# Joining the key tiles of the attention denominators on VectorE, and a later place for one denominator product

## The chip, the cores and the metric

The kernel runs on one NeuronCore of one Trainium2 chip. The metric is device time in microseconds (us): the median of several runs of the whole kernel, inputs and outputs in the chip's main memory. Smaller is better.

## The reference, cut to what matters

A forgetting attention (causal, with a decay made from the forget gates `f`) is followed by a two-layer MLP with a tanh GELU.

```
B, H, S, D = 8, 8, 576, 64;  scale = 1 / sqrt(64)
scores = scale * q @ k.T                        # per batch and head, 576 x 576
cum    = cumsum(log(clip(f, 1e-4, 1)))          # along the sequence
scores = where(causal, -1e9, scores + cum[query] - cum[key])
attn   = softmax(scores);  y = attn @ v         # y: (8, 8, 576, 64)
x      = y.transpose(0, 2, 1, 3).reshape(4608, 512)
out    = gelu_tanh(x @ w_in) @ w_out            # 512 -> 2048 -> 512, float32 out
```

In a row of the softmax the factor `exp(cum[query])` cancels. What is left is a weight per key, `w[key] = exp(-cum[key] - 64)`, on the exponential of the plain score: the output is `sum_k w[k] P[k,q] v[k] / sum_k w[k] P[k,q]` with `P = exp(scale * k.q)`, zero above the diagonal.

## The kernel before, in words

**Tiles.** The 64 pairs of batch and head are handled as 16 *quads* of 4 heads; quads 2b and 2b+1 belong to batch b. Keys lie on the 128 partitions, queries on the free axis, so `P` is stored transposed in `pt` (two buffers, quad i uses `pt[i % 2]`), 1536 columns a head: key tile 0 (keys 0-127) for queries 64-575, tile 1 for queries from 128 (448 columns), tile 2 from 256 (320 columns), tile 3 from 384 (192 columns), and one block of 64 columns that holds two halves, "low" (the first 64 keys for the first 64 queries) and "high" (the last 64 keys for the last 64 queries).

**One quad.** `scores` (L202-228) runs in three rounds of 512 columns; each fills two PSUM tiles of the pool `psS` (2 buffers) with matmuls of 32 rows, four heads side by side, and ScalarE writes the exponentials into `pt`, two heads at a time (L228). `mask` (L230-247) zeroes above the diagonals with `affine_select` on GpSimd (POOL). `make_vw` (L174-180) multiplies the values by `w`, also on POOL, behind the mask of round 1; `copy_low` (L182) copies a part of it on VectorE. `denominators(i)` (L297-313) multiplies `pt` by the weights `w_bf`: the function `product` (L266-293) issues 6 pieces x 4 heads = 24 matmuls, with four heads side by side on the columns of the array, and `den`, `rec`, `rb` on VectorE (transpose, reciprocal, transpose) turn the sums into factors. The columns streamed are 512 + 64 + 448 + 320 + 192 + 64 = 1600 a head. `attn_out(i, x)` (L315-319), twice a quad, is the same product with the 32 even or odd columns of the weighted values, and VectorE multiplies it by `rb` into `xT`. All these products use one PSUM buffer, `psO` (1 buffer), so each has to wait until VectorE has read the one before.

**The MLP.** It works on 9 chunks of 512 rows of `x`. `mlp_in` (L322-337) does 8 x 8 matmuls of 512 columns and a GELU on ScalarE; `mlp_out` (L357-376) is a generator that yields after each of 4 x 16 *parts* (a part is one 128-row step of a 128 x 512 output, here as four 32-column matmuls side by side). After every 16 parts VectorE copies the output tile to `o_st` (L373) and SyncE's queue stores it; `psM` has 2 buffers.

**The order** is written by hand; nothing plans it. Each engine takes its own instructions in program order. `setup` and the table `FRONT` handle quads 0-6; then the loop (L551-565) does, for chunk c from 2 to 6, first what is left of the output of chunk c-1, then the 8 groups of `mlp_in(c)` with `prepare` (transposes of q and k on VectorE and their next loads on POOL's queue) behind the second group, then 6 parts of output and `pair(i, j, c)` with i = 2c+3 and j = 2c+2. In `pair` (L524-536), which interleaves attention with parts of the output of chunk c, the order on TensorE is as follows (S = a score round, D = denominators, V = an output product, a number = parts of `mlp_out`, k = i+1):

```
S.i.0 D.j 12  S.i.1 V.j.0 10  S.i.2 V.j.1 9
S.k.0 D.i 10  S.k.1 V.i.0 5 V.i.1 4  S.k.2          (8 parts are left for the next chunk)
```

In the last pair (i = 15) there is no k: `S.i.0 D.j 12 S.i.1 V.j.0 10 S.i.2 V.j.1 9 D.i 10 V.i.0 V.i.1 10`.

Of the kernel before, what the change touches and what calls it, by code (L numbers as in the profile page):

```python
# [8 lines left out]
FP32 = mybir.dt.float32  # L9
BF16 = mybir.dt.bfloat16  # L10
AF = mybir.ActivationFunctionType
ALU = mybir.AluOpType
# [4 lines left out]
def kernel(  # L17
# [10 lines left out]
    nc = tc.nc  # L28

    B, H, S, D = q.shape  # L30
    BH = B * H
    NT = (S + 127) // 128
    LAST = S - 128 * (NT - 1)
# [7 lines left out]
    NQ = BH // 4  # L41
# [4 lines left out]
    CH = 512  # L46
    NCH = B * S // CH
    ZW = 64

    rounds = [(0, 512), (512, 512), (1024, 512)]  # L50
    pieces = [
# [28 lines left out]
        S.4.1 m.3.1 LQ.6 F.0.6 TQ.5 H.4.2.1 D.3 H.4.0.1 LQ.7 VW.4 H.4.0.0 V.3.1 v.3.0 f.0.3 H.4.2.0 CL.4 I.1.0 m.4.1 LV.2.1@LQ.5 I.1.5  # L80
        TQ.6 m.4.2.3 I.1.1 I.1.7 LV.3.0@LQ.7 m.4.2.2 TK.6 M.4.0 I.1.3 I.1.2 I.1.4 I.1.6 X F.1.8 S.5.0 F.1.2 F.1.14 S.5.1 D.4 M.5.0 f.1.9
        S.5.2 V.4.0 m.5.2.3 f.1.6 VW.5 V.4.1 CL.5 m.5.2.2 LQ.8 S.6.0 f.1.6 M.5.1 D.5 f.1.4 S.6.1 V.5.1 f.1.7 V.5.0 vw.6 S.6.2
        m.6.1 M.6.2.2 m.6.0 m.6.2.3 LK.7 LK.8 CL.6 LX.3.1@LK.6
    """

    singles = ctx.enter_context(tc.tile_pool(name="singles", bufs=1))
    ostage_pool = ctx.enter_context(tc.tile_pool(name="ostage", bufs=3))
# [5 lines left out]
    def many(n, shape, dtype, name):  # L93
        return [singles.tile(shape, dtype, name=f"{name}{i}") for i in range(n)]
# [19 lines left out]
    before = singles.tile([128, (NT - 1) * BH], FP32, name="before")  # L114
    wT = singles.tile([128, NQ, NT, 4], FP32, name="wT")
    w_bf = singles.tile([128, NQ, NT + 1, 4], BF16, name="w_bf")
    shift = singles.tile([128, 1], FP32, name="shift")
    idle = singles.tile([128, 512], BF16, name="idle")
    spare = singles.tile([1, 1], FP32, name="spare")
# [82 lines left out]
    def scores(i, r, groups=((0, 1, 2, 3),)):  # L202

        qq, p = qT[i % 2], pt[i % 2]
        if i < 2:
            off, n = split_rounds[r]
            todo = [(key, col - off, q0, nq) for (key, col, q0, nq) in split_pieces[r]]
        else:
            off, n = rounds[r]
            todo = []  # L210
            for (key, col, q0, nq) in pieces:
                a, z = max(col, off), min(col + nq, off + n)
                if a < z:
                    todo.append((key, a - off, q0 + a - col, z - a))
        for heads in groups:
            tiles = {g: psS.tile([128, 2, 512], FP32, name="ps_s", tag="s") for g in sorted({h // 2 for h in heads})}
            for c in range(2):
                for j, (key, c0, q0, nq) in enumerate(todo):
                    for h in heads:
                        nc.tensor.matmul(  # L220
                            tiles[h // 2][:, h % 2, c0:c0 + nq],
                            key_columns(i, key, h, c),
                            qq[32 * h:32 * h + 32, q0:q0 + nq, c],
                            start=(c == 0 and j == 0), stop=(c == 1),
                            skip_group_check=True,
                        )
            for g, t in tiles.items():
                nc.scalar.activation(p[:, 2 * g:2 * g + 2, off:off + n], t[:, :, 0:n], AF.Exp, scale=scale)  # L228
# [37 lines left out]
    def product(i, groups, spare, part=None):  # L266
        p = pt[i % 2]
        if part is not None:
            s0, s1 = parts[part]
            po = psM.tile([128, 512], FP32, name="po_m", tag="m")  # L270
            for (key, col, q0, nq) in sorted(sum(split_pieces[1:] if part else split_pieces[:1], []), key=lambda x: HIGH if x[0] == "high" else x[0]):
                for (r0, lhsT, h) in groups:
                    w = lhsT(HIGH if key == "high" else key)
                    nc.tensor.matmul(  # L274
                        po[r0:r0 + w.shape[-1], q0 - s0:q0 - s0 + nq], w, p[:, h, col:col + nq],
                        start=(key == 0), stop=(key == (HIGH if part else 1)),
                        skip_group_check=True,
                    )
            return po[:, 0:s1 - s0]
        if spare:  # L280
            po = psS.tile([128, 2, 512], FP32, name="ps_o", tag="s").rearrange("p a n -> p (a n)")
        else:
            po = psO.tile([128, 1024], FP32, name="po", tag="po")
        for (key, col, q0, nq) in sorted(pieces, key=lambda x: {0: 0, "low": 1}.get(x[0], 2)):
            t = {"low": LOW, "high": HIGH}.get(key, key)
            for (r0, lhsT, h) in groups:
                w = lhsT(t)
                nc.tensor.matmul(  # L288
                    po[r0:r0 + w.shape[-1], 448 + q0:448 + q0 + nq], w, p[:, h, col:col + nq],
                    start=(key in (0, "low")), stop=(key in ("low", "high")),  # L290
                    skip_group_check=True,
                )
        return po[:, 448:448 + S]

    rbs = {}

    def denominators(i, part=None):  # L297

        def column(h):

            return lambda t: (w_bf[:, i, t, h:h + 1] if t not in (0, LOW) else
                              w_bf[:, i, t, h:h + 1].to_broadcast([128, 32]))

        po = product(i, [(32 * h, column(h), h) for h in range(4)], False, part)
        n = S if part is None else parts[part][1] - parts[part][0]
        den = den_pool.tile([128, S], FP32, name="den", tag="den")
        nc.vector.transpose(out=den[:, 0:n], in_=po)  # L307
        rec = den_pool.tile([128, S // 32], FP32, name="rec", tag="rec")
        nc.vector.reciprocal(rec[:, 0:n // 32], den[:, 0:n:32])
        rb = den_pool.tile([128, S], FP32, name="rb", tag="rb")  # L310
        nc.vector.transpose(out=rb[:, 0:n].rearrange("p (c j) -> p c j", j=32),  # L311
                            in_=rec[:, 0:n // 32].unsqueeze(2).to_broadcast([128, n // 32, 32]))
        rbs[i, part] = rb[:, 0:n]

    def attn_out(i, x, spare=False, part=None):  # L315
        b, u = i // QPB, i % QPB
        po = product(i, [(32 * h, lambda t, h=h: vw[i % 2][:, t, h, x:D:2], h) for h in range(4)], spare, part)
        s0, s1 = (0, S) if part is None else parts[part]
        nc.vector.tensor_mul(xT[:, 2 * u + x, S * b + s0:S * b + s1], po, rbs[i, part])  # L319
# [106 lines left out]
    def make_w():  # L426
# [3 lines left out]
        for (rows, t0, t1) in ((128, 0, HIGH), (64, HIGH, NT)):  # L430
# [2 lines left out]
                cum_ps[:rows, t0 * BH:t1 * BH].rearrange("p (t i h) -> p t i h", i=NQ, h=4),  # L433
                AF.Exp, scale=-1.0, bias=shift[:rows, :])

    by_columns = []

    def pull(it, n):
# [7 lines left out]
    def out_part(c, n, tiled=0):  # L446
        by_columns[:] = [True] * tiled
        pull(fills.setdefault(c, mlp_out(c)), n)
# [5 lines left out]
    def load_values(b, half):  # L454
# [33 lines left out]
        "F": out_part,  # L488
        "f": lambda c, n: out_part(c, n, 1),
        "B": keep_busy,  # L490
        "X": load_exp,
    }

# [11 lines left out]
    def beside(i, r, c, todo):  # L505

        if i is not None:
            scores(i, r)
        for n, x in enumerate(todo):
            if isinstance(x, int):  # L510
                out_part(c, x, 1)
            else:
                x()
            if n == 0 and i is not None:
                after_scores(i, r)

    def after_scores(i, r):
        mask(i, r)
        if r == 1:
            make_vw(i, nc.gpsimd)  # L520
        if r == 2:
            copy_low(i)

    def pair(i, j, c):  # L524

        D, V = (lambda q: lambda: denominators(q)), (lambda q, x, spare=False: lambda: attn_out(q, x, spare))
        beside(i, 0, c, [D(j), 12])
        beside(i, 1, c, [V(j, 0), 10])
        beside(i, 2, c, [V(j, 1), 9])
        if i + 1 < NQ:  # L530
            beside(i + 1, 0, c, [D(i), 10])
            beside(i + 1, 1, c, [V(i, 0), 5, V(i, 1), 4])
            scores(i + 1, 2)
            after_scores(i + 1, 2)
        else:
            beside(None, 0, c, [D(i), 10, V(i, 0), V(i, 1, True), 10])

    def prepare(*quads):

        for i in quads:  # L540
            if i < NQ:
                transpose_k(i)
                transpose_q(i)
                if i + 2 < NQ:
                    load_one(k, k_c, i + 2)
                    load_one(q, q_c, i + 2)

    with tc.manual_schedule():
        setup()
        run(FRONT)  # L550
        for c in range(2, NCH):  # L551
            out_part(c - 1, CH)
            for pr in range(2):
                mlp_in(c, (pr,))
            if c + 1 < B:
                prepare(2 * c + 3, 2 * c + 4)
            if c + 2 < B:
                load_v(c + 2)
            for pr in range(2, NP):
                mlp_in(c, (pr,))  # L560
            if c + 1 < B:
                load_exp()
                out_part(c, 6)
                pair(2 * c + 3, 2 * c + 2, c)
        out_part(NCH - 1, CH)
# [30 lines left out]
```

## Time and profile before

| what | value |
|---|---|
| median of 3 runs | 341.61 us (341.45 to 345.22) |
| span of the profiled execution | 339.9 us, first to last instruction |
| around the span (median less span) | 1.7 us |
| TensorE (PE) busy | 329.8 us, 97% |
| VectorE (DVE) busy | 132.3 us, 39% |
| ScalarE (ACT) busy | 191.8 us, 56% |
| GpSimd (POOL) busy | 110.1 us, 32% |
| granted TensorE clock | 1.000 |

The page of the profile has, besides the busy time of each engine, the span cut into 40 slices with the busy tenths of each engine, the chain of work that ended last, and the costliest groups of instructions. The timeline of one engine gives start, duration, line, operation and `out<-in` of its instructions, neighbours of one kind merged (x3 stands for three instructions), and in brackets how long the engine sat idle before them and for whom. Durations of one instruction overlap with the next one's by the time an engine takes to drain, so the distance from start to start is shorter than the duration. The page gives the span of the profiled execution and no separate total for it; sums are made against the span of 339.9 us, and the 1.7 us around it are taken as they are.

### The profile page before, as it was taken

Reading aid. Unit: us, or ns where it says so; the run is one execution under the profiler, and the core shown is the slowest. Engines: PE = TensorE matmul, PEld = TensorE weight load, DVE = VectorE, ACT = ScalarE, POOL = GpSimd, SP = SyncE. Lnnn points to the kernel's source line nnn. Section 1 sums busy time; section 2 is a strip of 40 time slices with the busy share of each in tenths; the row PEclk is TensorE's granted clock in tenths of the full one; section 3 lists DMA queues with packets and bytes.
Section 4 is the critical chain, followed back from the end, with each engine's and each line's share of the span. In section 5 each row is a group of like instructions: output and inputs, shape, how many; then the busy total and the mean of one; then the engine's idle time right before and its main releaser. Section 6 shows DMA issues by size and latency. Waiting matters only on the chain.

```text
span 339.9 us, 9423 instructions
## 1 busy us (share of the span) xinstructions
PE 329.8 (97%) x4241; PEld 162.0 (48%) x4241; DVE 132.3 (39%) x206; ACT 191.8 (56%) x201; POOL 110.1 (32%) x155
## 2 busy tenths in 40 slices
PE   3999999999999999999999999999999999999996
PEld 1458844544454445444444444444544454444443
DVE  4686059830465435703462244413430450021011
ACT  4784686677547665667566665674576624502510
POOL 8987551600506233601551145106410410000000
PEclk9999999999999999999999999999999999999999
DMA  7999999570316970591129210910100010011012
GB/s 127 207 216 214 196 230 194 102 172 2 95 36 101 227 156 33 131 205 39 35 77 207 59 67 35 212 30 35 63 31 2 33 63 34 2 62 62 0 40 85
DMA packets 40201, 33.26 MB, mean 98 GB/s; under 512 B 27473, under 2 KB 29777, under 8 KB 40161
## 3 DMA queue, kind: packets, MB, share of 16 engines
q0 software_dynamic: 8848, 16.58, 27.4%
q1 hardware_dynamic: 31168, 16.01, 17.0%
q8 instruction: 33, 0.54, 0.7%
q10 hardware_dynamic: 144, 0.07, 0.1%
q14 instruction: 8, 0.06, 0.0%
HBM read 36.85 MB, written 9.44 MB: 136 GB/s over the span
## 4 chain that ended last, share of the span: by engine, by line
PE 90%; DMA 2%; POOL 2%; ACT 2%; DVE 1%; issue 1%; POOLq 0%; DVEq 0%; ACTq 0%
PE pso L368 36%; PE ps_h L330 33%; PE po L288 8%; PE ps_s L220 8%; PE ps_h L347 4%; DMA v_nat<-in_v_dram 2%; ACT pt L228 2%; PE po_m L274 1%; POOL vw L178 1%; POOL v_nat L132 0%; PE ps_o L288 0%; DVE pt L263 0%; DVE vw L178 0%; POOL pt L234 0%; POOL q_c L155 0%
## 5 line engine op out<-in xcount | busy, mean ns | idle before, releaser
L368 PE MATMUL pso<-w_out_sb,gT 128*32 128x512 bf16 (+3 forms) x1492 | 134.5, 377 | 0.0
L228 ACT ACTIVATE pt<-ps_s 128x1024 bf16<-128x1024 f32 (+2 forms) x100 | 93.7, 988 | 53.6 <-PE ps_s L220 46.0
L330 PE MATMUL ps_h<-xT,w_in_sb 128*128 128x512 bf16 x512 | 111.9, 379 | 0.0
L337 ACT ACTIVATE gT<-ps_h 128x1024 bf16<-128x1024 f32 x64 | 65.5, 1024 | 64.1 <-PE ps_h L330 64.1
L234 POOL TENSOR_SCALAR_AFFINE_SELECT pt<-pt 128x512 bf16<-128x512 bf16 (+3 forms) x65 | 38.2, 597 | 140.6 <-ACT pt L228 139.7
L368 PEld LDWEIGHTS <-gT 128*32 128x32 bf16 (+1 forms) x1492 | 56.3, 97 | 56.8 <-issue 3.5
L330 PEld LDWEIGHTS <-w_in_sb 128*128 128x128 bf16 x512 | 50.0, 98 | 60.4 <-issue 0.4
L373 DVE COPY o_st<-pso 128x512 f32<-128x512 f32 (+2 forms) x37 | 24.9, 673 | 71.8 <-PE pso L368 71.5
L307 DVE STREAM_TRANSPOSE den<-po 128x576 f32<-128x576 f32 x14 | 11.0, 784 | 65.7 <-PE po L288 65.7
L220 PE MATMUL ps_s<-qT,kT 32*128 32x64 bf16 (+5 forms) x896 | 36.2, 264 | 0.2 <-ACT pt L228 0.2
L319 DVE TENSOR_TENSOR xT<-po,rb 128x576 bf16<-128x576 f32 x26 | 19.7, 757 | 31.6 <-PE po L288 31.5
L178 POOL TENSOR_TENSOR vw<-v_nat,wT 128x1280 bf16<-128x1280 f32 (+1 forms) x13 | 30.0, 2308 | 0.1
L220 PEld LDWEIGHTS <-kT 32*128 32x128 bf16 x896 | 16.4, 93 | 23.7 <-issue 18.8
L161 DVE STREAM_TRANSPOSE kT<-k_c 128x576 f32<-128x576 f32 x16 | 20.0, 1248 | 16.9 <-DMA k_c<-in_k_dram 16.8
L288 PE MATMUL po<-pt,vw 128*32 128x64 bf16 (+4 forms) x624 | 22.4, 278 | 0.0
L161 DVE STREAM_TRANSPOSE qT<-q_c 128x576 f32<-128x576 f32 x16 | 19.9, 1244 | 1.2 <-PE ps_s L220 0.7
L288 PEld LDWEIGHTS <-vw 128*32 128x32 bf16 x672 | 14.2, 97 | 11.8 <-issue 3.7
L132 POOL DMA_DIRECT2D v_nat<-in_v_dram x20 | 15.3, 776 | 3.4 <-DMA w_out_sb<-in_moe_w_out_dram 3.4
L347 PE MATMUL ps_h<-xT,w_in_sb 128*128 128x256 bf16 x128 | 14.5, 273 | 0.0
L347 PEld LDWEIGHTS <-w_in_sb 128*128 128x128 bf16 x128 | 12.3, 98 | 1.7
L311 DVE STREAM_TRANSPOSE rb<-rec 128x576 f32<-128x576 f32 (+2 forms) x18 | 12.8, 711 | 0.6
L155 POOL DMA_DIRECT2D k_c<-in_k_dram x16 | 9.1, 568 | 11.3 <-DVE kT L161 5.7
(61 smaller groups left out, 124.9 us busy)
## 6 DMA issues: line engine op xcount, KB each, us to landing
out_dram<-o_st SPq DMA_DIRECT2D x35, 256.0 KB, 2.1
k_c<-in_k_dram POOLq DMA_DIRECT2D x16, 288.0 KB, 6.8
q_c<-in_q_dram POOLq DMA_DIRECT2D x16, 288.0 KB, 7.4
v_nat<-in_v_dram SPq DMA_DIRECT2D x16, 256.0 KB, 8.3
w_in_sb<-in_moe_w_in_dram POOLq DMA_DIRECT2D x4, 512.0 KB, 9.5
w_out_sb<-in_moe_w_out_dram POOLq DMA_DIRECT2D x4, 512.0 KB, 7.2
v_nat<-in_v_dram SPq DMA_DIRECT2D x16, 128.0 KB, 3.3
v_nat<-in_v_dram POOLq DMA_DIRECT2D x13, 128.0 KB, 7.9
```

Source lines behind the costliest of these rows:

```text
L161: nc.vector.transpose(out=dst.rearrange("p s c -> p (s c)").bitcast(FP32) .rearrange("p (t a) -> p a t", a=S // 32), in_=src.rearrange("p ...
L178: eng.tensor_mul(vw[i % 2][:, t0:t1], vb[:, t0:t1, h0:h0 + 4, :], wT[:, i, t0:t1, :].unsqueeze(3).to_broadcast([128, t1 - t0, 4, D]))
L220: nc.tensor.matmul(tiles[h // 2][:, h % 2, c0:c0 + nq], key_columns(i, key, h, c), qq[32 * h:32 * h + 32, q0:q0 + nq, c], start=(c == 0 an ...
L228: nc.scalar.activation(p[:, 2 * g:2 * g + 2, off:off + n], t[:, :, 0:n], AF.Exp, scale=scale)
L234: nc.gpsimd.affine_select(out=x, in_=x, compare_op=ALU.is_ge, fill=0.0, base=0, pattern=pattern, channel_multiplier=-1)
L288: nc.tensor.matmul(po[r0:r0 + w.shape[-1], 448 + q0:448 + q0 + nq], w, p[:, h, col:col + nq], start=(key in (0, "low")), stop=(key in ("lo ...
L319: nc.vector.tensor_mul(xT[:, 2 * u + x, S * b + s0:S * b + s1], po, rbs[i, part])
L330: nc.tensor.matmul(ph[:, j, :], w_in_sb[:, dt, 128 * ft:128 * ft + 128], xT[:, dt, CH * c:CH * (c + 1)], start=(dt == 0), stop=(dt == N_DT ...
L337: nc.scalar.activation(gT[c % 2][:, 2 * pr:2 * pr + 2, :], ph, AF.Gelu_apprx_tanh)
L347: nc.tensor.matmul(ph[:, j // 2, QA * (j % 2):QA * (j % 2) + QA], w_in_sb[:, dt, 128 * ft:128 * ft + 128], xT[:, dt, n0:n0 + QA], start=(d ...
L368: nc.tensor.matmul(pso[c0:c0 + cols, m0:m1], gT[c % 2][:, ft, 128 * n + c0:128 * n + c0 + cols], w_out_sb[:, ft, m0:m1], start=(ft == 0), ...
L373: nc.vector.tensor_copy(st[:, m0:m1], pso[:, m0:m1])
```

## The change

From quad 6 on, VectorE forms sums over key tiles before TensorE sees them. With `ratio[t] = w[tile t] / w[tile t+1]` per partition, `fold = P0 * ratio[0] + P1` is a tile for which the weight of tile 1 alone is enough; the same is done with tile 2 and tile 3 in place. `folded_sums` then multiplies each query range once, by the last tile that it has: 64 + 64 + 128 + 128 + 192 + 64 = 640 columns a head where there were 1600. Each fold of a quad is 4 instructions (one a head) of 448, 320 and 192 columns in turn. The even quads fold in the next chunk, ahead of `prepare`; the odd quad i of a pair folds inside the pair, and in the last pair only tile 0 is joined with tile 1 (1152 columns). All weights are now spread to 32 columns. `D.i` moves from behind S.k.0 to behind S.k.1, the parts are dealt out anew (none is left for the next chunk), and `V.i.1` moves behind S.k.2. In the new order below, E is a fold (E.i.0.0.1: quad i, tile 0 into 1, heads 0 and 1), and A is what follows a score round (mask, `make_vw`, `copy_low`).

```diff
+    PAIR = """
+        S.i.0 D.j A.i.0 12 S.i.1 V.j.0 A.i.1 E.i.0.0.1 10 S.i.2 V.j.1 A.i.2 E.i.0.2.3 9
+        S.k.0 E.i.1 E.i.2 A.k.0 12 S.k.1 D.i 6 V.i.0 A.k.1 6 S.k.2 V.i.1 A.k.2 4
+"""
+    LAST = """
+        S.i.0 D.j A.i.0 12 S.i.1 V.j.0 A.i.1 E.i.0.0.1 10 S.i.2 V.j.1 A.i.2 E.i.0.2.3 9
+        D.i 10 V.i.0 v.i.1 10
+"""
...
+    def fold_keys(i, t, heads=range(4)):
+        p, a = pt[i % 2], fold[i % 2]
+        q0, col = 128 * (t + 1), {0: 576, 1: 1024, 2: 1344}[t]
+        n = S - q0
+        for h in heads:
+            nc.vector.scalar_tensor_tensor(
+                a[:, h, q0 - 128:], p[:, h, 128:128 + n] if t == 0 else a[:, h, q0 - 128:],
+                ratio[:, i, t, h:h + 1], p[:, h, col:col + n], op0=ALU.mult, op1=ALU.add)
+        folded[i] = t + 1
+
+    def folded_sums(i, column, levels):
+        p, a = pt[i % 2], fold[i % 2]
+        po = psO.tile([128, 1024], FP32, name="po", tag="po")
+        todo = [(LOW, p[:, :, 0:64], 0), (0, p[:, :, 64:128], 64)]
+        for (t, q0, col, n) in ((1, 128, 576, 448), (2, 256, 1024, 320), (3, 384, 1344, 192)):
+            if t > levels:
+                todo.append((t, p[:, :, col:col + n], q0))
+            else:
+                z = S if t == levels else q0 + 128
+                todo.append((t, a[:, :, q0 - 128:z - 128], q0))
+        todo.append((HIGH, p[:, :, 0:64], 512))
...
     def denominators(i, part=None):
+        wide = range(NT + 1) if i in folded else (0, LOW)
...
-        po = product(i, [(32 * h, column(h), h) for h in range(4)], False, part)
+        if i in folded:
+            po = folded_sums(i, column, folded[i])
+        else:
+            po = product(i, [(32 * h, column(h), h) for h in range(4)], False, part)
...
+    def make_ratio():                 # once, at the end of FRONT
+        r = ratio[:, FOLD:]           # FOLD = 6
+        nc.vector.reciprocal(r, wT[:, FOLD:, 1:NT - 1, :])
+        nc.vector.tensor_mul(r, r, wT[:, FOLD:, 0:NT - 2, :])
...
             if c + 1 < B:
+                for t in range(3):
+                    fold_keys(2 * c + 2, t)
                 prepare(2 * c + 3, 2 * c + 4)
```

More of the change, by code (lines that the diff above doesn't have):

```diff
@@ L48 @@
     ZW = 64
+    FOLD = 6
     rounds = [(0, 512), (512, 512), (1024, 512)]
@@ L82 @@
         S.5.2 V.4.0 m.5.2.3 f.1.6 VW.5 V.4.1 CL.5 m.5.2.2 LQ.8 S.6.0 f.1.6 M.5.1 D.5 f.1.4 S.6.1 V.5.1 f.1.7 V.5.0 vw.6 S.6.2
-        m.6.1 M.6.2.2 m.6.0 m.6.2.3 LK.7 LK.8 CL.6 LX.3.1@LK.6
+        m.6.1 M.6.2.2 m.6.0 m.6.2.3 LK.7 LK.8 CL.6 LX.3.1@LK.6 RA
     """
+    PAIR = """
[6 more added lines that the diff above has]
+"""
     singles = ctx.enter_context(tc.tile_pool(name="singles", bufs=1))
@@ L116 @@
     w_bf = singles.tile([128, NQ, NT + 1, 4], BF16, name="w_bf")
+    ratio = singles.tile([128, NQ, NT - 2, 4], FP32, name="ratio")
+    fold = many(2, [128, 4, S - 128], BF16, "fold")
     shift = singles.tile([128, 1], FP32, name="shift")
@@ L295 @@
     rbs = {}
+    folded = {}
+    def fold_keys(i, t, heads=range(4)):
[18 more added lines that the diff above has]
+        todo.append((HIGH, p[:, :, 0:64], 512))
+        for j, (t, x, q0) in enumerate(todo):
+            for h in range(4):
+                w = column(h)(t)
+                nc.tensor.matmul(
+                    po[32 * h:32 * h + w.shape[-1], 448 + q0:448 + q0 + x.shape[-1]], w, x[:, h, :],
+                    start=(j < 2), stop=(j in (0, len(todo) - 1)), skip_group_check=True)
+        return po[:, 448:448 + S]
     def denominators(i, part=None):
+        wide = range(NT + 1) if i in folded else (0, LOW)
         def column(h):
-            return lambda t: (w_bf[:, i, t, h:h + 1] if t not in (0, LOW) else
+            return lambda t: (w_bf[:, i, t, h:h + 1] if t not in wide else
                               w_bf[:, i, t, h:h + 1].to_broadcast([128, 32]))
-        po = product(i, [(32 * h, column(h), h) for h in range(4)], False, part)
+        if i in folded:
+            po = folded_sums(i, column, folded[i])
+        else:
+            po = product(i, [(32 * h, column(h), h) for h in range(4)], False, part)
         n = S if part is None else parts[part][1] - parts[part][0]
@@ L490 @@
         "B": keep_busy,
+        "RA": make_ratio,
         "X": load_exp,
@@ L524, in pair @@
     def pair(i, j, c):
[L526 to L536, printed above, removed]
+        last = i + 1 == NQ
+        for word in (LAST if last else PAIR).split():
+            name, *args = word.split(".")
+            if name.isdigit():
+                out_part(c, int(name), 1)
+                continue
+            q, *args = args
+            q = {"i": i, "j": j, "k": i + 1}[q]
+            args = list(map(int, args))
+            if name == "A":
+                after_scores(q, *args)
+            elif name == "E":
+                fold_keys(q, args[0], args[1:] or range(4))
+            else:
+                ops[name](q, *args)
     def prepare(*quads):
```

## The prediction

> **What bounds the kernel now.** First the page: busy time, then the chain that ended last.
>
> ```profile
> span 339.9 us, 9423 instructions
> PE 329.8 (97%) x4241; PEld 162.0 (48%) x4241; DVE 132.3 (39%) x206; ACT 191.8 (56%) x201; POOL 110.1 (32%) x155
> ...
> PE 90%; DMA 2%; POOL 2%; ACT 2%; DVE 1%; issue 1%; POOLq 0%; DVEq 0%; ACTq 0%
> ```
>
> TensorE is the bound, without gaps from pair to pair, so a column taken from it is a gain, and any wait put before it is a loss at full price. VectorE's 39% hides nothing by itself: what matters is where in a pair its work stands. So I read one pair, (i, j) = (11, 10), in the chain (start, duration, what):
>
> ```profile
> 190.37 0.62 PE ps_s L220 x20
> 190.99 0.80 PE po L288 x24
> 191.79 2.59 PE pso L368 x48
> ...
> 201.20 0.63 PE ps_s L220 x21
> 201.83 0.80 PE po L288 x24
> 202.63 2.16 PE pso L368 x40
> 204.78 0.57 PE ps_s L220 x16
> ```
>
> A product (`po`, 24 matmuls) costs 0.80 behind a score round, 12 parts 2.59 (0.216 a part). The whole period, from one `mlp_in` to the next, is 35.9 us (175.26 to 211.17). Next POOL's and VectorE's timelines in the same pair, and the place where the two meet:
>
> ```profile
> 197.10 0.64 POOL L234 TENSOR_SCALAR_AFFINE_SELECT pt<-pt 128x512 bf16<-128x512 bf16 x1 [2.44 <-ACT pt L228]
> 197.71 2.33 POOL L178 TENSOR_TENSOR vw<-v_nat,wT 128x1280 bf16<-128x1280 f32 x1
> 200.59 1.23 POOL L234 TENSOR_SCALAR_AFFINE_SELECT pt<-pt 128x512 bf16<-128x512 bf16 x2 [0.55 <-ACT pt L228]
> 203.96 1.14 POOL L234 TENSOR_SCALAR_AFFINE_SELECT pt<-pt 64x256 bf16<-64x256 bf16 x2 [2.14 <-ACT pt L228]
> ```
>
> ```profile
> 103.17 0.42 DVE L263 TENSOR_TENSOR pt<-pt,causal 128x512 bf16<-128x512 bf16 x1
> ```
>
> ```profile
> 103.50 1.19 DVE L263 TENSOR_TENSOR pt<-pt,causal 128x512 bf16<-128x512 bf16 x2
> ```
>
> ```profile
> 103.69 0.72 POOL L234 TENSOR_SCALAR_AFFINE_SELECT pt<-pt 128x512 bf16<-128x512 bf16 x1 [13.16 <-ACT pt L228]
> ```
>
> The last three are the key. Three equal VectorE multiplications with two SBUF inputs follow each other. Alone one takes 0.42; the second and third, with a POOL mask between them, take 1.19 together, where 0.34 + 0.42 would do. The mask ends at 104.41, the third at 104.69: it stood still until POOL was through. An instruction with two SBUF inputs waits here for a POOL instruction that reads SBUF. A fold is of that kind, and so are the neighbours that it gets.
>
> **Part 1, TensorE's gain.** Ten quads (6 to 15) change. Nine stream 640 columns in place of 1600. At 0.216 us for 512 columns that is 960 x 0.216 / 512 = 0.405 us each, the tenth (1152 columns) 0.19: together **-3.8 us**. Steps of 64 columns now stand one behind another; in the product at 190.92 the step behind a 64-column step follows 0.03 us after it, so short steps keep the pace, with weights of 32 columns too (the output products have these). The moved `D.i`, `V.i.1` and the 8 parts are the same work elsewhere: 0. Dealing all 64 parts out in the pair takes away nothing that the bound waits for: at the seam to `mlp_in` the first psS tile is free when S.k.2's first exponential ends, some 1.65 us behind that round's start, and V.i.1 plus 3 parts reach to 2.0; slack 0.3.
>
> **Part 2, the folds' length.** No row shows this operation. From both sides: one element a cycle, as the rows with two f32 inputs have it (1280 elements at 101.77, next start at 103.17: 1.40 us; with 64 fixed steps that is (n + 64) / 960), or two a cycle, as the bf16 multiplication above (0.34 from start to start for 512). So 448, 320 and 192 columns cost 0.53, 0.40, 0.27 or 0.30, 0.23, 0.17; a quad 4.8 or 2.8 us. I take the slow end: scaling and adding in one pass has more to do than the one multiplication that runs at the fast rate. [...] The even quad's folds (4.8 us) and the four transposes behind them (4.4) end some 11 us into `mlp_in`, which has 13.8 and 1.3 of parts behind it; two of the transposes are all that S.i.0 needs. The loads behind them on POOL's queue start about 6 us later than now and are wanted a period later: 0. `make_ratio`, two instructions of 120 elements, 0.5 us once beside `mlp_in`: 0.
>
> **Part 3, where the odd quad's folds end up.** Zero is the start of S.i.0. TensorE without a stall, from the durations above: S.i.1 3.61, V.j.0 4.17, S.i.2 7.13, V.j.1 7.70, S.k.0 10.43, 12 parts 11.07, S.k.1 13.66, **D.i 14.22**. From the rows, the masks come 2.7 us behind the start of their round: mask i.1 6.33-6.97, then at once vw 6.94-9.27; masks i.2 from 9.82; masks k.0 from 13.19. VectorE in program order:
> - E.i.0 heads 0, 1 wait for mask i.1 (6.97). vw, which reads SBUF, is already under way: they stand until 9.2, then 2 x 0.53 = 10.25.
> - The multiplication of V.j.1 (ready at 8.55) waits behind them: 10.95. Nobody is late: the next user of psO is now D.i.
> - Masks i.2 got in behind the second fold, about 10.2-11.4. The small copy, then E.i.0 heads 2, 3: 11.4-12.5; the output copy 0.61: 13.1.
> - E.i.1, 4 x 0.40, and E.i.2, 4 x 0.27, would end at 15.8. But masks k.0 (1.14 us) want in at 13.19, as the mask at 103.69 did between two VectorE instructions: and each holds VectorE for its length less the 0.14 or so by which the third multiplication above overlapped the mask's end: 0.27 + 0.55, so 16.6.
>
> D.i needs E.i.2 for its fifth step and would have ended at 14.63; it now ends 0.15 behind E.i.2, at about 16.75. **Stall 2.1 us** (1.3 if the masks stay outside until the folds are done, 2.4 if POOL also gets the first turn at 13.19). Behind the stall stand `den` (one output copy first), V.i.0 after 6 parts, and the rest of the pair; by the same steps none of these is late again. So a full pair costs 2.1 - 0.81 = +1.3, and four of them +5.2. In the last pair D.i waits only for E.i.0, visible at 12.6, and 448 + 320 + 192 + 64 columns follow: end 13.1, against 11.6 now (273.81 less 262.19): +1.4 with D.j's gain in it. Sum **+6.6 us**: span 346.5, and with the 1.7 around it about **348.2**. [...]
>
> **The rivals.**
> 1. *The folds don't wait for POOL* (not slower). With one element a cycle: E.i.0 first half 7.0-8.1, V.j.1's multiplication 8.55-9.25, copy, second half 9.5-10.6, output copy 11.2, E.i.1 12.8, E.i.2 13.9. D.i at 14.22 finds all done, 0.3 to spare, and the whole -3.8 stays: 337.8. For it: the order fits this almost to the tenth. Against it: the 1.19. It decides from the first fold on: if that starts at 7.0 and not at 9.2.
> 2. *Half of it*: either vw lets a fold in (only the masks block), or folds run two elements a cycle. Then E.i.2 ends at about 15.0 or 14.7, D.i stalls 0.3 to 0.6, each pair gains 0.2 to 0.5, the last loses 0.1 to 0.4: -0.7 to -1.7, 340 to 341. No row shows vw against a VectorE start in its middle.
> 3. *The short steps don't stream*: loading 32 columns of weights for a 64- or 128-column step is not hidden and D costs what it did: +3.8 on top of the forecast, 352.0. Against it the 0.03 us steps.
> 4. *The folds cost more than the slow end*, a fixed cost of 0.1 us for the per-partition ratio: 12 x 0.1 more in front of D.i, +4 to +6 on the forecast.
>
> **How the numbers follow.** Forecast 0.50, rival 1 0.18, rival 2 0.20, rival 3 0.04, rival 4 0.08. The range takes in the forecast and rivals 1 and 2, 337.5 to 350.5, with 0.12 left above it; the forecast's own range is 345 (stall 1.3) to 350. 2% is 6.8 us, about what a measurement of this kernel can tell from no change: slower means over 348.4, which is not quite half of the forecast and all of rivals 3 and 4: 0.34. Faster means under 334.8, out of reach of the 3.8 us: 0.02. Within 2%: 0.64.
>
> **What the profile after would show.** Right: PE idle about 2 us in each pair inside D.i, ended by VectorE's fold, and `po<-fold` matmuls of 128 and 192 columns; first folds with durations near 2.7 us that end with vw; masks k.0 longer than 1.14; VectorE busy at 180 to 200 us. Wrong: no PE idle before D.i (rival 1), folds of 448 columns at 0.4 us (rival 2), D intervals of 0.8 where nothing waits (rival 3). The forecast falls if the wait that the rows at 103.50 show does not hold for a fold, or for vw, or if the edges where POOL and VectorE alternate cost much less than a whole instruction.

## The result, and the profile after

The changed kernel takes **354.35 us** (median of 6 runs, 353.71 to 355.72) against 341.57 for the kernel before (6 runs): ratio 1.0363, 95% interval 1.0319 to 1.0406. It is slower by 12.8 us; the forecast was 348.2, in a range to 350.5. The direction was right, the size was about half of what came.

The busy times and the chain's shares by engine on the page of the changed kernel:

```profile
span 352.5 us, 9746 instructions
PE 334.5 (95%) x4315; PEld 168.0 (48%) x4337; DVE 201.8 (57%) x320; ACT 191.8 (54%) x201; POOL 114.5 (32%) x155
...
PE 78%; DVE 11%; issue 5%; POOL 3%; ACT 2%; POOLq 0%; ACTq 0%
```

TensorE carried 90% of the chain before and carries 78% now; VectorE, which had 1%, has 11%. The chain of the pair (13, 12), in order of time (start, duration, what), shows where; the shortest pieces are left out. Zero of the prediction's count is 234.79.

```profile
234.79 0.63 PE ps_s L233 x24
235.82 2.59 PE pso L418 x48
238.41 0.62 PE ps_s L233 x13
239.11 0.88 issue
239.99 1.03 ACT pt L241
241.14 0.65 POOL pt L247
241.81 2.34 DVE fold L317
245.08 0.74 DVE xT L369
245.86 0.47 DVE vw L196
246.35 0.74 DVE fold L317 x2
247.55 0.69 DVE o_st L423
248.24 0.61 DVE fold L317 x2
248.85 0.73 issue
249.58 1.07 DVE fold L317 x3
250.83 1.45 DVE fold L317 x3
252.54 1.35 PE pso L418 x22
```

From mask i.1 on (241.14) the chain has left TensorE: first fold, multiplication of V.j.1, small copy, folds, output copy, folds, and only then TensorE again, at the end of D.i (252.5). That is the queue of VectorE that the prediction wrote out, link by link. The same pair in the timelines of POOL and VectorE:

```profile
241.14 0.64 POOL L247 TENSOR_SCALAR_AFFINE_SELECT pt<-pt 128x512 bf16<-128x512 bf16 x1 [2.04 <-ACT pt L241]
241.75 2.33 POOL L191 TENSOR_TENSOR vw<-v_nat,wT 128x1280 bf16<-128x1280 f32 x1
244.68 1.57 POOL L247 TENSOR_SCALAR_AFFINE_SELECT pt<-pt 128x512 bf16<-128x512 bf16 x2 [0.60 <-ACT pt L241]
248.04 1.28 POOL L247 TENSOR_SCALAR_AFFINE_SELECT pt<-pt 64x256 bf16<-64x256 bf16 x2 [1.80 <-ACT pt L241]
251.42 0.64 POOL L247 TENSOR_SCALAR_AFFINE_SELECT pt<-pt 128x512 bf16<-128x512 bf16 x1 [2.10 <-ACT pt L241]
```

```profile
241.81 3.35 DVE L317 SCALAR_TENSOR_TENSOR fold<-pt,ratio 128x448 bf16<-128x448 bf16 x2 [1.23 <-POOL pt L247]
245.08 0.74 DVE L369 TENSOR_TENSOR xT<-po,rb 128x576 bf16<-128x576 f32 x1
245.86 0.47 DVE L196 COPY vw<-vw 64x256 bf16<-64x256 bf16 x1
246.35 1.28 DVE L317 SCALAR_TENSOR_TENSOR fold<-pt,ratio 128x448 bf16<-128x448 bf16 x2
247.55 0.69 DVE L423 COPY o_st<-pso 128x512 f32<-128x512 f32 x1
248.15 4.12 DVE L317 SCALAR_TENSOR_TENSOR fold<-fold,ratio,pt 128x320 bf16<-128x320 bf16 x8
```

Two folds of 448 columns take 1.28 us at 246.35, where POOL is still, and 3.35 at 241.81, where vw starts 0.06 before them: the first one lasts 2.75 (241.81 to 244.56), until 0.5 behind the end of vw (244.08). Eight shorter folds need 4.12 with three masks among them. And TensorE, at the place where it waits:

```profile
249.26 0.28 PE L337 MATMUL po<-fold,w_bf 128*32 128x128 bf16 x5
249.71 0.22 PE L337 MATMUL po<-fold,w_bf 128*32 128x128 bf16 x1 [0.18 <-DVE fold L317]
250.17 0.22 PE L337 MATMUL po<-fold,w_bf 128*32 128x128 bf16 x1 [0.25 <-DVE fold L317]
250.63 1.23 PE L337 MATMUL po<-fold,w_bf 128*32 128x128 bf16 x4 [0.25 <-DVE fold L317]
252.33 0.24 PE L337 MATMUL po<-fold,w_bf 128*32 128x192 bf16 x1 [0.46 <-DVE fold L317]
```

D.i's matmuls come one by one, each when a fold ends. D.i ends at 252.44 or 17.65 in the prediction's count, against 14.63 without a wait: a stall of 3.0 us, where 2.1 were forecast.

The periods from one `mlp_in` to the next, read from the starts of its first matmul, put the whole result together:

| pair | before | after | difference | forecast |
|---|---|---|---|---|
| (7, 6) | 35.91 | 37.82 | +1.9 | +1.3 |
| (9, 8) | 35.91 | 39.97 | +4.1 | +1.3 |
| (11, 10) | 35.91 | 38.29 | +2.4 | +1.3 |
| (13, 12) | 35.91 | 38.30 | +2.4 | +1.3 |
| (15, 14) | 34.19 | 35.89 | +1.7 | +1.4 |

The sum is +12.4 of the 12.6 between the two spans (339.9 and 352.5); the forecast's sum was +6.6. Two pairs are cases of their own. In (7, 6) the last fold starts just before mask k.1 and not behind it. The first two lines are its last two folds and that mask, the third is the same two folds in the pair (13, 12), where the mask of 251.42 comes first:

```profile
134.98 0.73 DVE L317 SCALAR_TENSOR_TENSOR fold<-fold,ratio,pt 128x192 bf16<-128x192 bf16 x2
135.32 0.89 POOL L247 TENSOR_SCALAR_AFFINE_SELECT pt<-pt 128x512 bf16<-128x512 bf16 x1 [2.19 <-ACT pt L241]
...
251.16 1.11 DVE L317 SCALAR_TENSOR_TENSOR fold<-fold,ratio,pt 128x192 bf16<-128x192 bf16 x2
```

Here the mask waits and the folds are 0.38 us shorter, which is most of what this pair loses less than the others. The other case is (9, 8). The stretches below are its stall and what follows, then the same place cut where the clock changes (length, then busy time of PE, PEld, DVE, ACT and POOL, then the granted clock, and two columns on DMA):

```profile
170.92:174.17 3.25, 1.84 (x32) 0.84 (x32) 3.25 (x8) 1.94 (x2) 1.15 (x3) 1.00 0.20 74
174.17:181.23 7.06, 7.06 (x130) 4.43 (x124) 3.46 (x6) 1.21 (x2) 2.02 (x1) 0.76 0.11 39
...
171.59:175.00 3.41, 2.17 (x30) 1.19 (x32) 3.41 (x8) 1.44 (x2) 1.84 (x2) 1.00 0.00 1
175.00:178.41 3.41, 3.41 (x51) 2.47 (x47) 2.10 (x4) 0.00 (x0) 1.19 (x1) 0.50 0.22 82
```

Behind the stall TensorE ran 3.41 us at half its clock (175.00 to 178.41), and that pair lost 39.97 - 38.29 = 1.7 us more than its neighbours.

### The profile page after: what moved, and what is told of

It is laid out like the page before. It is cut to its first block, busy times and chain, and to the rows that moved or that the text cites. A ratio compares the mean times of both kernels' runs of the same rounds, so it can differ in the third digit from the quotient of the medians.

```text
span 352.5 us, 9746 instructions
## 1 busy us (share of the span) xinstructions
PE 334.5 (95%) x4315; PEld 168.0 (48%) x4337; DVE 201.8 (57%) x320; ACT 191.8 (54%) x201; POOL 114.5 (32%) x155
## 4 chain that ended last, share of the span: by engine, by line
PE 78%; DVE 11%; issue 5%; POOL 3%; ACT 2%; POOLq 0%; ACTq 0%
PE ps_h L380 31%; PE pso L418 27%; DVE fold L317 8%; PE ps_s L233 7%; PE po L301 4%; PE ps_h L397 4%; ACT pt L241 2%; PE po_m L287 1%; POOL pt L247 1%; PE idle_ps L212 1%; DVE xT L369 1%; PE po L337 1%; DVE o_st L423 1%; POOL v_nat L145 1%; DVE vw L196 1%
## 5 line engine op out<-in xcount | busy, mean ns | idle before, releaser
L418 PEld LDWEIGHTS <-gT 128*32 128x32 bf16 (+1 forms) x1588 | 60.5, 98 | 55.4 <-issue 4.4
L247 POOL TENSOR_SCALAR_AFFINE_SELECT pt<-pt 128x512 bf16<-128x512 bf16 (+3 forms) x65 | 42.3, 659 | 125.8 <-ACT pt L241 122.9
L380 PEld LDWEIGHTS <-w_in_sb 128*128 128x128 bf16 x512 | 49.8, 98 | 61.1 <-issue 2.1
L317 DVE SCALAR_TENSOR_TENSOR fold<-pt,ratio 128x448 bf16<-128x448 bf16 x40 | 37.3, 983 | 6.3 <-POOL pt L247 6.1
L317 DVE SCALAR_TENSOR_TENSOR fold<-fold,ratio,pt 128x320 bf16<-128x320 bf16 (+1 forms) x72 | 32.2, 516 | 0.0
L301 PE MATMUL po<-pt,vw 128*32 128x64 bf16 (+4 forms) x624 | 23.6, 284 | 0.0
L301 PEld LDWEIGHTS <-vw 128*32 128x32 bf16 x672 | 16.1, 98 | 11.0 <-issue 3.7
L337 PE MATMUL po<-fold,w_bf 128*32 128x128 bf16 (+2 forms) x112 | 10.5, 232 | 6.2 <-DVE fold L317 4.9
```

The costliest lines, as they stand in the source:

```text
L247: nc.gpsimd.affine_select(out=x, in_=x, compare_op=ALU.is_ge, fill=0.0, base=0, pattern=pattern, channel_multiplier=-1)
L301: nc.tensor.matmul(po[r0:r0 + w.shape[-1], 448 + q0:448 + q0 + nq], w, p[:, h, col:col + nq], start=(key in (0, "low")), stop=(key in ("lo ...
L317: nc.vector.scalar_tensor_tensor(a[:, h, q0 - 128:], p[:, h, 128:128 + n] if t == 0 else a[:, h, q0 - 128:], ratio[:, i, t, h:h + 1], p[:, ...
L380: nc.tensor.matmul(ph[:, j, :], w_in_sb[:, dt, 128 * ft:128 * ft + 128], xT[:, dt, CH * c:CH * (c + 1)], start=(dt == 0), stop=(dt == N_DT ...
L418: nc.tensor.matmul(pso[c0:c0 + cols, m0:m1], gT[c % 2][:, ft, 128 * n + c0:128 * n + c0 + cols], w_out_sb[:, ft, m0:m1], start=(ft == 0), ...
```

## The experiments

Theory A: the folds stand behind POOL instructions that read SBUF, and D.i stands behind the folds. Theory B: 12 folds are simply too much VectorE work for that place, whatever POOL does. Theory C: the new order costs time by itself.

### The new order without folds

```diff
     def fold_keys(i, t, heads=range(4)):
+        return
```

> The new order of the pairs without any fold; the denominators are made from pt as before, and make_ratio is there without a reader. Theory A (the folds stand behind POOL instructions that read SBUF, and D.i waits for the folds) and theory B (the folds are too long for their place whatever POOL does): the order by itself is free, 341 to 342.5 us, no idle time of TensorE in a pair. Theory C (the move of D.i and V.i.1 and the 64 parts in the pair cost time): several us above 341.6.

Measured: 342.33 us, ratio 1.0031 (1.0011 to 1.0052). Its periods are 36.03 against 35.91: 0.12 us a pair, small but there in each of the four. Theory C falls as an explanation of 12.8 us; the 36.03 is the mark from which the folds' own gain is to be counted. What makes the 0.12 was not tried.

### vw out of the way

```diff
-        if r == 1:
+        if r == 1 and i % 2 == 0:
             make_vw(i, nc.gpsimd)
-        if r == 2:
+        if r == 2 and i % 2 == 0:
             copy_low(i)
...
                 prepare(2 * c + 3, 2 * c + 4)
+                make_vw(2 * c + 3, nc.gpsimd)
+                copy_low(2 * c + 3)
```

> The changed kernel, with vw of the odd quad (and the small copy that follows it) made behind prepare, while mlp_in runs, and not behind mask i.1; all else stays. Theory A: the first fold lasts about 0.67 us and not 2.75; the masks i.2 and k.0 still get in between, so D.i's stall falls from 3.0 to about 0.8 us a pair, and the kernel comes to 341 to 343 us. Theory B: what VectorE does before D.i is as long as before, the stall stays near 3 us and the time near 354.

Measured: 341.97 us, ratio to the kernel before 1.0016 (1.0003 to 1.0029). Full pairs take 36.00 in place of 38.29 us. In the timeline of VectorE the folds that follow mask i.1 now read:

```profile
233.36 1.28 DVE L317 SCALAR_TENSOR_TENSOR fold<-pt,ratio 128x448 bf16<-128x448 bf16 x2 [1.22 <-POOL pt L247]
...
235.57 1.27 DVE L317 SCALAR_TENSOR_TENSOR fold<-pt,ratio 128x448 bf16<-128x448 bf16 x2
...
237.37 4.16 DVE L317 SCALAR_TENSOR_TENSOR fold<-fold,ratio,pt 128x320 bf16<-128x320 bf16 x8
```

1.28 and not 3.35; the same folds, the same masks (the last eight still take 4.16, with the masks of k.0 among them), and 2.3 us less in the pair. Of the wait that the folds bring, the 2.3 us are three quarters. They are not vw's alone: the small copy on VectorE, 0.47 us in the changed kernel, left the place with it. Theory B wanted no change here, and falls.

### No POOL reader beside the folds

```diff
     def after_scores(i, r):        # on top of the edit above
-        mask(i, r)
+        if i % 2 == 0 and r > 0:
+            mask(i, r)
```

> As the run before, and all masks of the odd quads and that of round 0 of the even quads (from quad 7 on) are left out, so that no POOL instruction reads SBUF between S.i.0 and the mask of round 1 of k; the causal mask is missing there, and the output is not the reference's. Theory A: all 12 folds run at 0.60, 0.46 and 0.33 us from start to start, the last ends before D.i needs it, no stall, the gain of 3.8 us shows: 337 to 339. Theory B: a stall of 2 us or more is left in each pair, over 345.

Measured: 338.15 us, ratio 0.9905 (0.989 to 0.992). Periods 35.23 us, TensorE waits for no fold. So with POOL out of the way (the folds have no mask i.1 to wait for here either; the next run has it) the 12 folds fit: against the order alone (36.03) a pair gains 0.80, which is what two products of 0.405 less were to bring.

### A version that keeps POOL apart

```diff
-  S.i.0 D.j A.i.0 12 S.i.1 V.j.0 A.i.1 E.i.0.0.1 10 S.i.2 V.j.1 A.i.2 E.i.0.2.3 9
-  S.k.0 E.i.1 E.i.2 A.k.0 12 S.k.1 D.i 6 V.i.0 A.k.1 6 S.k.2 V.i.1 A.k.2 4
+  S.i.0 D.j A.i.0 12 S.i.1 V.j.0 A.i.1 E.i.0 10 S.i.2 V.j.1 A.i.2 9
+  S.k.0 E.i.1 E.i.2 12 S.k.1 D.i 6 V.i.0 A.k.1 A.k.0 6 S.k.2 V.i.1 A.k.2 4
```

The same edit of E.i.0 is made in the last pair, and vw of the odd quad is made early as above.

> A full kernel: vw of the odd quad made while mlp_in runs, the four folds of tile 0 in one piece behind mask i.1, and the masks of k.0 put behind mask k.1 and vw of k, so that POOL reads nothing while the folds run, but for the masks i.2. Theory A: D.i finds its folds done or waits under 0.3 us; 337 to 339, faster than both kernels, and the granted clock stays at 1.000. Theory B: VectorE's work before D.i is the same, 350 or more.

Measured: **338.51 us**, ratio to the kernel before 0.9913 (0.9898 to 0.9927): the fastest of the full kernels, 3.0 us under the kernel before and 15.8 under the changed one. Periods 35.23, granted clock 1.000. VectorE in the pair (13, 12):

```profile
231.23 2.47 DVE L317 SCALAR_TENSOR_TENSOR fold<-pt,ratio 128x448 bf16<-128x448 bf16 x4 [1.21 <-POOL pt L247]
233.62 0.75 DVE L369 TENSOR_TENSOR xT<-po,rb 128x576 bf16<-128x576 f32 x1
234.29 0.68 DVE L423 COPY o_st<-pso 128x512 f32<-128x512 f32 x1
234.89 3.50 DVE L317 SCALAR_TENSOR_TENSOR fold<-fold,ratio,pt 128x320 bf16<-128x320 bf16 x8
```

and D.i on TensorE, through in one go:

```profile
237.93 0.64 PE L233 MATMUL ps_s<-qT,kT 32*128 32x64 bf16 x16
238.50 0.24 PE L337 MATMUL po<-pt,w_bf 128*32 128x64 bf16 x8
...
238.79 1.47 PE L418 MATMUL pso<-w_out_sb,gT 128*32 128x512 bf16 x24
```

Four folds of 448 run in 2.47 us in one piece, the other eight in 3.50 where the changed kernel takes 4.12, and D.i reaches from 238.50 to 238.79: 0.29 us, with no gap.

### Only the masks of k.0 moved

```diff
-  S.k.0 E.i.1 E.i.2 A.k.0 12 S.k.1 D.i 6 V.i.0 A.k.1 6 S.k.2 V.i.1 A.k.2 4
+  S.k.0 E.i.1 E.i.2 12 S.k.1 D.i 6 V.i.0 A.k.1 A.k.0 6 S.k.2 V.i.1 A.k.2 4
```

> The changed kernel with one difference: the masks of round 0 of k stand behind mask k.1 and vw of k, so that they no longer come between the folds E.i.1 and E.i.2. vw of the odd quad stays where it is. Theory A (vw costs the most): the first fold keeps its 2.75 us, the stall before the end of D.i falls from 3.0 to about 2.2 us a pair, 350 to 352 us. Were the masks k.0 the main thing, the time would come near 342.

Measured: 349.40 us, ratio 1.0235 (1.022 to 1.025), a little under the range given. Periods 37.41 in all four full pairs, 0.88 us under the changed kernel's 38.29, and no stretch at half clock: the 1.7 us of that stretch are gone too, and the expectation says nothing of them. Moving vw alone gave 2.29, moving these masks alone 0.88; both together, with the four folds of tile 0 in one piece, gave 3.06.

### Short folds

```diff
-            nc.vector.scalar_tensor_tensor(a[...], ..., ratio[...], p[...], op0=ALU.mult, op1=ALU.add)
+            nc.vector.tensor_add(a[...], ..., p[...])
```

> The changed kernel with each fold a plain bf16 addition of the two tiles (tensor_tensor in place of scalar_tensor_tensor); the ratio of the weights is left out, so the denominators are not the reference's. POOL's work is untouched. By the rows of the kernel before, a fold then takes 0.30, 0.23 and 0.17 us from start to start, 2.8 us a quad and not 5.5. Theory A: the first fold still waits for vw and lasts about 2.4 us; D.i's stall falls to 0.2 to 0.6 us; 338.5 to 341 us. A theory in which only POOL's waits count and the length of the folds does not: the stall stays near 2.3, over 348.

Measured: 341.01 us, ratio 0.9976 (0.9951 to 1.0001), at the upper end of the range given. POOL's work and the order are those of the changed kernel. On VectorE, same place:

```profile
232.27 2.82 DVE L317 TENSOR_TENSOR fold<-pt 128x448 bf16<-128x448 bf16 x2 [1.22 <-POOL pt L247]
...
236.47 0.69 DVE L317 TENSOR_TENSOR fold<-pt 128x448 bf16<-128x448 bf16 x2
...
237.68 2.36 DVE L317 TENSOR_TENSOR fold<-fold,pt 128x320 bf16<-128x320 bf16 x8
```

The first pair of folds takes 2.82, not 0.69 as the second pair: a plain addition waits for vw too, so the wait is not the new operation's. But the rest of the queue is so much shorter that three of the four full pairs take 35.61 us, 0.38 over the free 35.23, and the first takes 35.21. So neither cause alone makes the loss: the wait for POOL is there with short folds too, and the long folds are harmless without POOL. It takes both for VectorE to arrive 3 us late.

### TensorE kept busy in the stall

```diff
-  ... 12 S.k.1 D.i 6 V.i.0 ...
+  ... 12 S.k.1 B.i D.i 6 V.i.0 ...        # B: 12 matmuls of 512 columns on zeros
```

> The changed kernel with 12 matmuls of 512 columns on zeros put in front of D.i in the four full pairs, 2.6 us of useless work for TensorE in the place where it stands and waits. If the half-speed stretch of 3.4 us that one pair of the changed kernel shows comes from that standing still, it is gone: granted clock 1.000 after the start, about 1.7 us less than the changed kernel, 352 to 353 us, although work was added. If the stretch has another cause, it stays, and the time is 354 to 356.

Measured: 352.77 us, ratio to the kernel before 1.0334 (1.0319 to 1.035): 1.6 us less than the changed kernel with 48 matmuls more. The pair (9, 8) is now like its neighbours (the four full pairs take 38.15, 38.29, 38.29, 38.30) and the granted clock is 1.000 in all four timed runs; the changed kernel has 0.990 to 0.995 in all six.

### A longer stall

```diff
-  S.k.0 E.i.1 E.i.2 A.k.0 12 ...
+  S.k.0 E.i.1 G.i E.i.2 A.k.0 12 ...      # G: 4 more folds of 448 into an unread tile
```

> The changed kernel with 4 more folds of 448 columns (into a tile that nobody reads) between E.i.1 and E.i.2 in the four full pairs, 2.4 us more on VectorE in front of D.i. If TensorE's clock falls after a long stand, more pairs than one show a stretch at half speed, and each pair loses 2.4 us, up to 2.3 more if a fold falls behind vw of k, and some 1.7 where the clock falls: 366 to 380 us. If the clock has nothing to do with it, still one stretch or none, 364 to 373.

Measured: 377.79 us (two runs), above the 373 at which the range without a falling clock ended, mean clock 0.959. In its first full pair TensorE stands like this:

```profile
133.81 0.22 PE L338 MATMUL po<-fold,w_bf 128*32 128x128 bf16 x1 [0.25 <-DVE fold L318]
138.97 1.30 PE L338 MATMUL po<-fold,w_bf 128*32 128x192 bf16 x4 [4.94 <-DVE fold L318]
```

The trace has one stretch at half clock in each of the four full pairs, of 10.24, 6.83, 6.83 and 6.83 us: three and two times 3.41.

## Why the prediction was wrong, point by point

**What held.** The bound, the place and the mechanism: the first fold behind vw (forecast to start at 9.2 of the pair and end at 9.7; its end is 244.56 - 234.79 = 9.8), V.j.1's multiplication behind it without harm, masks among the folds, D.i late and everything behind D.i in time. Part 1's 0.405 us a product is 0.80 a pair in the run without masks. The first fold's 2.75 us show that vw blocks a fold as a mask does, which no row showed beforehand: that it would was the author's estimate from a mask of 0.72 us. They refute rival 1 and the first half of rival 2. The other half falls because a fold of 448 columns takes 0.60 us from start to start, where two elements a cycle were to give 0.30, and rival 3 by D.i's 0.29 us.

**Where it failed: the length of a fold, Part 2.** The sum took (n + 64) / 960 us, which fits rows of plain two-input operations. The kernel before has a second such row beside the 1.40 us for 1280 elements, 0.67 from start to start for 576:

```profile
206.21 0.76 DVE L319 TENSOR_TENSOR xT<-po,rb 128x576 bf16<-128x576 f32 x1 [1.63 <-PE po L288]
206.88 0.68 DVE L373 COPY o_st<-pso 128x512 f32<-128x512 f32 x1
```

704 elements more cost 0.73 us, about 1/960 us each (the "cycle" of the prediction, and a step here), and what is left is about 0.067 us, 64 such steps. That a fold would run at this rate was the author's choice of the slow end, and no row before showed it. Start to start, the undisturbed folds are 0.60, 0.46 and 0.33 us for 448, 320 and 192 columns (246.35 to 246.96, 250.04 to 250.50, 250.83 to 251.16): one element in 1/960 us, as assumed, but 124 fixed steps, since (448 + 124) / 960 is 0.60. That is 60 steps or 0.0625 us more for each of 12 folds, 0.75 us a pair and 3.0 us in the four full pairs, all of it in front of D.i. Rival 4 named this as a fixed cost of 0.1 us and +4 to +6 us on the forecast; it was given 8%, and it is about half of the 6.1 us by which the result lies over the forecast. The row that was chosen shows an operation with no operand read per partition, and its fixed part was carried over as if it were the same. In the run with short folds the plain additions fit the 64 steps: two folds of 448 columns take 236.47 to 237.08, 0.30 us each, which is (448/2 + 64) / 960. Whether the operand per partition makes the other 60, or the second operation in one pass, no run separates.

**What followed from it, Part 3.** With the folds later by that much, the last one met mask k.1 too, which the forecast had ending behind them: at 251.42 POOL takes its 0.64 and the last fold lasts 0.78 in place of 0.41, 0.38 us more. The pair (7, 6), where the fold came first, shows this share by itself: it loses 1.9 and not 2.4. In the other direction, the two masks k.0 cost less than the 0.82 of the forecast: the first two folds of 320 columns reach from 248.15 to 249.58, 1.43 us where two undisturbed ones need 0.93, so 0.50. 0.75 + 0.38 - 0.32 is 0.81 of the 0.9 us by which the stall is longer than forecast. With the 0.12 for the order, which the prediction put at 0, it is 0.93 of the 1.1 between 1.3 and 2.4 us a pair; the rest is assigned to nothing. In the last pair +1.7 came for +1.4.

**What was not seen at all: the clock.** The sum has no term for it. 1.7 us of the 12.6 between the spans of the two profiled executions are one stretch at half clock behind a stall. That the standing still causes it is shown from both sides: it goes when the stall is filled with useless matmuls (granted clock 1.000 in all four runs), and comes in every pair when the stall is made longer (0.959).

**The sum as measured.** 1.9 + 2.4 x 3 + 1.7 = 10.8 for the pairs, where 6.6 was forecast, and 1.7 for the clock: 12.5 of the 12.6 us between the spans. The range ended at 350.5 because the two sizes that were carried over from other operations, the fixed part of a fold and the margin to mask k.1, were taken as values and not as bounds. An end of the range at "each fold 0.1 us longer, and one more mask met" would have been about 354.5 (348.2 + 4 x 1.2 + 4 x 0.38). The chances leaned the other way: 0.64 lay on a change within 2%, and 0.34 on a slower kernel, which came.

## What to carry to other kernels

An engine that is 39% busy is no place for 5 us of work until the queue around it is written out with everything that can hold it, and two engines that hold each other up count as one there: the same folds cost 12.8 us beside POOL's vw and masks, and bring 3.0 where vw and the masks k.0 are moved to stretches in which VectorE has no instruction with two SBUF inputs (only the masks i.2 stay beside the folds). Work that depends on nothing new (vw needs only values and weights) is the first to be moved out of such a place. When a new operation stands before the bound a dozen times, its fixed part is worth as much care as its rate.

## What the runs showed of the hardware

- In all five pairs of the changed kernel, the first fold, a VectorE instruction with two SBUF inputs, starts 0.06 to 0.07 us behind the start of vw, a POOL instruction that reads SBUF, and stands: it lasts 2.75 us where 0.67 is its own length. In the pair (13, 12) it ends at 244.56, so its own 0.67 would begin at 243.89, 0.2 us before vw ends (244.08). The plain addition did the same (first two folds 2.82 in place of 0.69), and it shows the other way round too: the mask at 244.68 lasts 0.98 behind a running fold, 0.64 alone. The small bf16 copy on VectorE, with one SBUF input, also took 0.47 beside a mask and 0.22 alone.
- After a stall of 3 us in which short matmuls still ran one by one, with no gap over 0.46 us, TensorE fell to half clock in one pair of four; in the run with the longer stall, where the gap in the first pair is 4.94 us, it fell in every pair. The stretches are 3.41 us, or two or three times that. What sets the one pair of four apart can be read from the trace of the changed kernel. Its record of the clock starts at 14.57 at full speed, falls at 175.00 and rises at 178.41: 160.43 and 3.41 us, or 47 steps and one step of 3.413, so the steps counted from 14.57 make a grid on which both changes lie. An estimate of how long TensorE streams columns in a step (0.216 us for 512 columns, overlaps counted once) gives 1.29 us for the step from 171.59 to 175.00 in the pair (9, 8), at whose end the clock falls, although TensorE was not idle in it. In the pair (13, 12) a stall of the same length lies otherwise on the grid, its thinnest step (250.09 to 253.50) still has 1.53 us, and the clock stays. By the same estimate every other step of this trace up to 349.07, where the matmuls have ended, has 1.79 us or more. No step lies between 1.29 and 1.53, so where a border is, if it is there at all, remains open.
- In D.i of the run that keeps POOL apart, 24 matmuls of 64 to 192 columns, four side by side with a weight load of 32 columns each, stream 640 columns in 0.29 us, where 0.216 us for 512 columns would give 0.27: these short steps cost hardly more than their columns.
